# Sliding-window attention on half-array tiles: plain transposed queries, 64-row products, nine rows per partition, and one slot order for all pairs

## The chip, the core and the metric

The kernel runs on one core of one Trainium2 chip. The core has a matrix engine (TensorE; PE in the profile, PEld for its weight loads), VectorE (DVE), ScalarE (ACT), GpSimd (POOL) and a queue engine (SP). Each engine works through its own instructions in order; semaphores tie them together. 16 DMA engines move data between HBM and the core's memory SBUF. Matrix products land in PSUM, eight banks of 2 KB per partition, and VectorE and ScalarE read them from there. The metric is the device time of one execution in microseconds (us).

## What is computed

The reference is causal attention with a window of 64 positions, and behind it a mixture-of-experts layer with soft slots:

```python
# q, k, v: batch 8, heads 8, sequence 576, head size 64, fp32
scores = scale * q @ k.T                       # per batch and head
mask = (rel >= 0) & (rel < 64)                 # rel = query position - key position
attn = softmax(where(mask, scores, -1e9))
x = attn @ v                                   # -> 4608 tokens x 512
logits = x @ phi                               # 512 x 32 slots (8 experts, 4 slots each)
d = softmax(logits, over tokens)
slot_input = d.T @ x                           # 32 x 512
slot_out[e] = relu(slot_input[e] @ w1[e]) @ w2[e]     # 512 -> 1024 -> 512
out = softmax(logits, over slots) @ slot_out   # 4608 x 512, fp32
```

About 28 MB of q, k and v and 33.5 MB of weights are read, and 9.4 MB are written.

## The kernel before

**Pairs and blocks.** The 64 (batch, head) combinations are handled as 32 pairs of neighbouring heads. The sequence is cut into nine blocks of 64 queries; a block of queries sees a window of 128 keys (its own 64 and the 64 before). A window product is therefore 64 queries by 128 keys, for two heads.

**Loading and turning.** `load_rows` (L75) brings q or k of two pairs with one GpSimd DMA that casts to fp16. 96 partitions hold six consecutive rows each, four heads beside one another (RQ = 6, RP = 96). `st_transpose` (L315) turns one pair with twelve transposes of 96x64 into a PSUM bank, a_q for q and a_k for k: head 0 comes out on partitions 0 to 63 and head 1 on 64 to 127. `st_copy_k` (L325) copies k into `kT` (128 partitions by 64+576) on ScalarE, on VectorE in every fourth slot. `st_copy_q` (L332) copies q in two ScalarE instructions of 64 partitions each into `qb`, which is block diagonal: each block of 128 columns has 64 columns of head 0 (zeros on the other head's partitions) and 64 of head 1. `zero_q` writes the zeros once.

**Products.** With the block-diagonal q one 128x128 product gives both heads. `st_max` (L347) puts the mask (`wm`, by a product with the identity, two of 512 columns) and eight window products into the two banks of a_m; `st_max_read` takes the maximum of each query on VectorE. `st_max8` does the ninth block, `st_shift` turns the maxima so that they become rows of `rt`, and VectorE copies them there (L370). `st_scores` (L372) then forms the transposed scores in a_s, eight 128x128 products and eight more with `lh` and `rt` that add mask and shift; `st_exp` takes the exponential of all eight blocks in one ScalarE instruction. The ninth block has a place of its own in the bank a_k (`st_score8`, `st_exp8`). `st_av` multiplies with v, 18 products of 128x64, into a_v, and `st_norm` divides on VectorE and writes x_b.

**Behind the attention of a batch.** `fr_transpose` and `fr_transpose_copy` turn x_b into xt (PE into a_k, ScalarE out of it). After four pairs come logits (`fr_logits`, bank a_q), their running maximum (`fr_max`), exponentials (`fr_exp`), a transpose (`fr_dispatch`), the slot sums (`fr_slots`) and their accumulation (`fr_acc`, VectorE); the softmax over slots is `fr_turn`, `cb_max`, `cb_sub` (GpSimd), `cb_exp`, `cb_turn`.

**Order.** The program's order is the order on every engine. The loop over slots n = -1 to 30 handles k of pair n+1, q of pair n, maxima of n-1, shift and scores of n-2, the ninth block of n-3 and v of n-4. The work of a batch is spread by lags: in slot n the call `of(n, lag)` names the batch whose first pair is n-lag. What the last pairs still need is written out by hand behind the loop (L680 to L755). Then the experts run: `first` (L815) makes the hidden layer, `second` and `second_last` the output of the experts in two halves of 256 columns, `give` multiplies with the slot softmax, scales and writes to HBM.

**Queues.** All loads but the first rows and phi are issued by GpSimd in program order (`loads`, L542), between its own copies: `shift_v` (L176) makes a copy of v shifted by 64 rows. q and k groups have four buffers each; WSLOTS says in which slots a weight of 2 MB is issued. PSUM is used up by single buffers: a_m, a_v and a_s have two banks, a_k and a_q one, so a bank is written again only when its reader is done.

Of the kernel before, what the change touches and what calls it, by code (L numbers as in the profile page):

```python
# [18 lines left out]
def kernel(  # L19
# [47 lines left out]
    RQ = 6  # L67
    RP = S // RQ
    assert RP == 96
# [5 lines left out]
    def load_rows(src, g, tag, pairs=(0, 1)):  # L75
        t = pin.tile([128, 4, RQ * Dh], FP16, name=tag, tag=tag)
        b, gq = divmod(g, 2)
        h0, nh = 4 * gq + 2 * pairs[0], 2 * len(pairs)
        nc.gpsimd.dma_start(out=t[0:RP, 0:nh, :],  # L79
                            in_=src[b].rearrange("h (p r) d -> p h (r d)", p=RP)[:, h0:h0 + nh, :])  # L80
        for i, pr in enumerate(pairs):
            staged[tag, 2 * g + pr] = t, 2 * i
# [17 lines left out]
    for i, (src, tag, pr) in enumerate(((k, "ks", 0), (q, "qs", 0), (k, "ks", 1), (q, "qs", 1))):  # L100
        f = w1_t[5 - i // 2, 0][:, :, :].rearrange("p c f -> p (c f)").bitcast(FP32)
        f = f[0:RP, 768 * (i % 2):768 * (i % 2) + 768].rearrange("p (h x) -> p h x", h=2)
        nc.sync.dma_start(out=f, in_=src[0].rearrange("h (p r) d -> p h (r d)", p=RP)[:, 2 * pr:2 * pr + 2, :])
        if pr == 0:
            staged[tag] = pin.tile([128, 4, RQ * Dh], FP16, name=tag, tag=tag)
        first_rows[tag, pr] = f
        staged[tag, pr] = staged[tag], 2 * pr

    def round_rows(tag, pr, copy):
        copy(out=staged[tag][0:RP, 2 * pr:2 * pr + 2, :], in_=first_rows[tag, pr])  # L110
# [105 lines left out]
    NK, NQ = 4, 3  # L216
    kTs = [pqk.tile([128, 64 + S], FP16, name=f"kT{i}") for i in range(NK)]
    qbs = [pqk.tile([128, NB, 2, 64], FP16, name=f"qb{i}") for i in range(NQ)]
    def zero_q(i):
        nc.vector.memset(qbs[i][64:128, :, 0, :], 0.0)  # L220
        nc.vector.memset(qbs[i][0:64, :, 1, :], 0.0)
# [3 lines left out]
    zero_q(0)  # L225
# [16 lines left out]
    def make_rt(rt):  # L242
        nc.vector.tensor_copy(out=rt[64:128, :], in_=db[64:128, 11:12].broadcast_to([64, 128]))
        nc.vector.tensor_copy(out=rt[0:64, 0:64], in_=ident_h[0:64, 0:64])
        nc.vector.tensor_copy(out=rt[0:64, 64:128], in_=ident_h[0:64, 0:64])
# [19 lines left out]
    def late_constants(n):  # L265
        if n == 0:
            nc.vector.memset(ms[0], 0.0)
            zero_q(1)
        elif n == 1:
            nc.vector.tensor_tensor(out=lh[64:128, 0, 0:64], in0=lh[64:128, 0, 0:64],  # L270
                                    in1=db[64:128, 10:11].broadcast_to([64, 64]), op=ALU.add)
            make_rt(rts[0])
            nc.vector.memset(ms[1], 0.0)
            zero_q(2)
        elif n == 2:
            make_rt(rts[1])
        elif n == 3:
# [35 lines left out]


    def st_transpose(p, tag, tq):  # L315
        src, h = staged[tag, p]
        for r in range(RQ):
            for hf in range(2):
                nc.tensor.transpose(tq[64 * hf:64 * hf + 64, RP * r:RP * r + RP],  # L319
                                    src[0:RP, h + hf, Dh * r:Dh * r + Dh], ident_h[0:RP, 0:RP])  # L320
# [4 lines left out]
    def st_copy_k(p, on_vector=False):  # L325
        if on_vector:
            nc.vector.tensor_scalar(out=kTs[p % NK][:, 64:64 + S], in0=turned(a_kh), scalar1=QKS, scalar2=None,  # L327
                                    op0=ALU.mult)
        else:
            nc.scalar.activation(kTs[p % NK][:, 64:64 + S], turned(a_kh), AF.Copy, scale=QKS)  # L330

    def st_copy_q(p, both=False):  # L332
        for hf in range(2):
            h = slice(64 * hf, 64 * hf + 64)
            if hf and both:
                nc.vector.tensor_scalar(out=qbs[p % NQ][h, :, hf, :], in0=turned(a_qh)[h], scalar1=QKS, scalar2=None,  # L336
                                        op0=ALU.mult)
            else:
                nc.scalar.activation(qbs[p % NQ][h, :, hf, :], turned(a_qh)[h], AF.Copy, scale=QKS)  # L339

    def qblock(p, i):
        return qbs[p % NQ][:, i, :, :].rearrange("p l x -> p (l x)")

    def kwindow(p, i):
        return kTs[p % NK][:, 64 * i:64 * i + 128]

    def st_max(p):  # L347
        for j in range(2):
            nc.tensor.matmul(a_m[:, j, :], ident_h[:, :], wm[:, j:j + 4, :].rearrange("p c x -> p (c x)"),  # L349
                             start=True, stop=False, skip_group_check=True)  # L350
        for i in range(8):
            nc.tensor.matmul(a_m[:, i // 4, 128 * (i % 4):128 * (i % 4) + 128], qblock(p, i), kwindow(p, i),  # L352
                             start=False, stop=True, skip_group_check=True)
# [4 lines left out]

    m8 = a_v[:, 0, 384:512]

    def st_max8(p, m8=m8):
        nc.tensor.matmul(m8, ident_h[:, :], wm[:, 1, :], start=True, stop=False, skip_group_check=True)
        nc.tensor.matmul(m8, qblock(p, 8), kwindow(p, 8), start=False, stop=True, skip_group_check=True)

    def st_max8_read(p, m8=m8):
        nc.vector.reduce_max(ms[p % 2][:, 72:73], m8, axis=AXX)  # L366

    def st_shift(p, t_=a_v[:, 1, 384:512]):
# [3 lines left out]
    def st_scores(p, blocks, at):  # L372
        rt = rts[p % NR]
        for i in blocks:
            nc.tensor.matmul(at(i), kwindow(p, i), qblock(p, i), start=(i % 4 == 0), stop=False,  # L375
                             skip_group_check=True)
        for i in blocks:
            nc.tensor.matmul(at(i), lh[:, i, :], rt[:, :], start=False, stop=True, skip_group_check=True)  # L378

    def st_score(p):  # L380
        st_scores(p, range(8), lambda i: a_s[:, i // 4, 128 * (i % 4):128 * (i % 4) + 128])

    def st_exp(p):
        nc.scalar.activation(st_pt(p)[:, 0:8, :].rearrange("p i x -> p (i x)"), a_s[:, :, :], AF.Exp, scale=XS)  # L384

    s8 = a_k[:, 288:416]

    def st_score8(p):
        st_scores(p, (8,), lambda i: s8)

    def st_pt(p):
        if p not in pts:
            pts[p] = pw.tile([128, NB, 128], FP16, name="pt", tag="pt")
        return pts[p]

    def st_exp8(p):
        nc.scalar.activation(st_pt(p)[:, 8, :], s8, AF.Exp, scale=XS)

    def st_av(p, a_v=a_v):
# [3 lines left out]
        for hf in range(2):  # L403
            for i in range(NB):
# [4 lines left out]
                                 pt[:, i, 64 * hf:64 * hf + 64], rhs, start=True, stop=True, skip_group_check=True)  # L409

    def st_norm(p, a_v=a_v):
# [120 lines left out]
    WSLOTS = {16 * i // 5: i for i in range(10)}  # L532
    WSLOTS.update({NP - 2: 10, NP - 1: 11})

# [7 lines left out]
    def loads(n):  # L542
# [6 lines left out]
        elif i > 0:  # L549
# [5 lines left out]

    for n in range(-1, NP - 1):
        loads(n)
        lb, eb, sb, cb = [of(n, lag) for lag in range(8, 12)]
        if of(n, 12) is not None:
            cb_sub(of(n, 12), nc.gpsimd)  # L560
        def maxima():
            st_max(n - 1)
            st_max8(n - 1)
            if live(n - 2):
                st_shift(n - 2)
            st_max_read(n - 1)
            st_max8_read(n - 1)

        early = n < 4
        if live(n - 3) and not early:  # L570
            st_score8(n - 3)
        if early and live(n - 1):
            maxima()
        if n == 0:
            warm_up(1)
        if live(n - 3) and early:
            st_score8(n - 3)
        if early and live(n):
            st_transpose(n, "qs", a_qh)
            st_copy_q(n, n == 0)  # L580
        if n == 0:
            warm_up(2)
            round_rows("qs", 1, nc.scalar.copy)

        kv = n == 2 or n % 4 == 1 and not early
        if live(n + 1):
            st_transpose(n + 1, "ks", a_kh)
        if live(n - 3):
            st_exp8(n - 3)
        if live(n + 1) and not kv:  # L590
            st_copy_k(n + 1)
        if live(n - 4):
            st_av(n - 4)
        if live(n) and not early:
            st_transpose(n, "qs", a_qh)
        if lb is not None:
            fr_logits(lb)
        if live(n) and not early:
            st_copy_q(n)
        if eb is not None:  # L600
            fr_exp(eb)
        if lb is not None:
            fr_logits_copy(lb)
        if live(n - 4):
            st_norm(n - 4)
        if live(n + 1) and kv:
            st_copy_k(n + 1, True)

        if live(n - 1) and not early:
            maxima()  # L610
        if live(n - 4):
            fr_transpose(n - 4)
            fr_transpose_copy(n - 4)
        if of(n, 15) is not None:
            cb_exp(of(n, 15))
        if live(n - 2):
            st_score(n - 2)
# [352 lines left out]
```

## Time and profile before

| what | value |
|---|---|
| time, median of 3 runs | 190.93 us (190.47 to 191.08) |
| time of the profiled execution | 190.24 us |
| its span, first to last instruction | 188.2 us |
| busy: PE, DVE, ACT, POOL | 160.0, 142.9, 145.0, 83.0 us |
| granted TensorE clock, mean | 0.978 |
| read from HBM, written | 61.93 MB, 9.44 MB |
| exponentials of pairs 0, 8, 28, 31 start at | 13.80, 45.77, 130.30, 140.68 us |
| first product of the experts starts at | 150.31 us |

Busy time is a share of time with something in work, not of peak. Matrix products are pipelined: one takes some 200 ns from start to end, but the next may start 56 ns later (128 columns), so groups of products are read by the distance of their starts. The name in front of a line number is the tile that is written; "<-" in a row of waits names who ended the wait.

### The profile page before, as it was taken

What the parts mean: (1) busy time and instruction counts of PE and PEld (TensorE: products, weight loads), DVE (VectorE), ACT (ScalarE), POOL (GpSimd) and SP (SyncE); (2) the same over time, 40 slices, a digit from 0 to 9 for tenths busy, and PEclk for the clock granted to TensorE, in tenths of its full rate; (3) what the DMA queues carried; (4) which work ended last, traced back from release to release, by engine and by line L of the source; (5) the groups of instructions that cost most, each with busy time, mean ns of one, the idle gap of its engine ahead of it and who ended that gap; (6) DMA issues with size and microseconds to landing.
All of it is one profiled execution on the core that took longest, in us unless ns stands there. A gap on an engine that the chain in (4) does not pass through costs nothing.

```text
span 188.2 us, 7073 instructions
## 1 busy us (share of the span) xinstructions
PE 160.0 (85%) x3039; PEld 120.5 (64%) x3039; DVE 142.9 (76%) x354; ACT 145.0 (77%) x267; POOL 83.0 (44%) x123
## 2 busy tenths in 40 slices
PE   5777999999999999999999999999899899878400
PEld 1466778877777677777777787777785357543100
DVE  6797786897888789788888878897887734689700
ACT  6677879989889899889898898989478455589500
POOL 7955726171682453862953706707653170000000
PEclk9999999999999999999999999999999999999965
DMA  6999999999999999999999999999999999999996
GB/s 160 223 184 185 228 172 226 175 222 180 185 223 180 213 191 185 201 206 181 209 193 191 211 187 190 203 202 192 216 211 216 205 196 193 247 340 392 417 417 264
DMA packets 62302, 41.47 MB, mean 220 GB/s; under 512 B 38848, under 2 KB 58304, under 8 KB 61376
## 3 DMA queue, kind: packets, MB, share of 16 engines
q0 software_dynamic: 56560, 30.35, 116.7%
q1 hardware_dynamic: 5712, 10.68, 16.0%
q8 instruction: 23, 0.38, 0.7%
q14 instruction: 7, 0.06, 0.1%
HBM read 61.93 MB, written 9.44 MB: 379 GB/s over the span
## 4 chain that ended last, share of the span: by engine, by line
PE 45%; DVE 34%; ACT 6%; DMA 5%; issue 4%; DVEq 0%; SPq 0%; ACTq 0%
DVE m L356 10%; PE a_m L349 5%; DVE x_b L418 5%; PE a_m L352 5%; PE a_v L408 4%; PE a_s L375 4%; PE a_s L378 4%; PE a_q L319 3%; DMA out_dram<-w 3%; PE a_k L432 3%; DVE kT L327 3%; DVE rt L370 2%; DVE acc L529 2%; DMA w<-in_q_dram 2%; PE ha L819 2%
## 5 line engine op out<-in xcount | busy, mean ns | idle before, releaser
L339 ACT ACTIVATE qb<-a_q 64x576 f16<-64x576 f16 x63 | 40.6, 645 | 6.1 <-PE a_q L319 4.9
L356 DVE TENSOR_REDUCE m<-a_m 128x8 f16<-128x1024 f32 x32 | 39.1, 1223 | 1.0
L384 ACT ACTIVATE pt<-a_s 128x1024 f16<-128x1024 f32 x32 | 32.8, 1023 | 6.8 <-PE a_s L378 5.6
L183 POOL COPY v<-v 64x576 int32<-64x576 int32 x16 | 10.6, 661 | 41.1 <-DMA v<-in_v_dram 41.0
L418 DVE TENSOR_TENSOR x_b<-a_v,rc 128x640 f16<-128x640 f32 x31 | 25.6, 824 | 1.1
L352 PEld LDWEIGHTS <-qb 128*128 128x128 f16 x256 | 16.9, 98 | 7.6 <-DVE qb L336 0.3
L349 PE MATMUL a_m<-wm,ident_h 128*128 128x512 f16 x64 | 19.3, 384 | 1.4 <-DVE m L356 1.4
L378 PEld LDWEIGHTS <-lh 128*128 128x128 f16 x288 | 18.7, 98 | 2.0 <-issue 1.7
L173 POOL DMA_DIRECT2D v<-in_v_dram x16 | 19.7, 1234 | 0.0
L375 PEld LDWEIGHTS <-kT 128*128 128x128 f16 x288 | 18.6, 98 | 1.6 <-issue 1.4
L436 ACT COPY xt<-a_k 128x576 f16<-128x576 f16 x28 | 17.9, 639 | 2.2 <-PE a_k L432 0.9
L375 PE MATMUL a_s<-qb,kT 128*128 128x128 f16 x256 | 19.5, 219 | 0.0
L378 PE MATMUL a_s<-rt,lh 128*128 128x128 f16 x256 | 19.5, 219 | 0.0
L352 PE MATMUL a_m<-kT,qb 128*128 128x128 f16 x256 | 19.5, 219 | 0.0
L408 PE MATMUL a_v<-v,pt 128*64 128x65 f16 x558 | 15.6, 196 | 2.4 <-DVE m L366 1.1
L79 POOL DMA_DIRECT2D ks<-in_k_dram x15 | 10.5, 697 | 16.0 <-PE a_s L378 3.8
L370 DVE CAST rt<-a_v 9x128 f16<-9x128 f32 x30 | 8.7, 289 | 10.8 <-PE a_v L369 10.5
L408 PEld LDWEIGHTS <-pt 128*64 128x64 f16 x576 | 13.5, 110 | 4.7 <-DVE m L366 1.8
L330 ACT ACTIVATE kT<-a_k 128x576 f16<-128x576 f16 x24 | 15.7, 655 | 0.8 <-PE a_k L319 0.8
L319 PE MATMUL a_q<-ident_h,qs 96*64 96x96 f16 x384 | 14.8, 206 | 1.2 <-DVE a_q L228 1.1
L319 PE MATMUL a_k<-ident_h,ks 96*64 96x96 f16 x384 | 14.4, 212 | 1.0 <-DVE ks L110 0.8
L901 DVE TENSOR_SCALAR w<-cp,rcs 128x256 f32<-128x256 f32 (+1 forms) x24 | 13.4, 610 | 2.3 <-PE cp L896 1.9
(183 smaller groups left out, 327.8 us busy)
## 6 DMA issues: line engine op xcount, KB each, us to landing
w<-in_moe_w_dram POOLq DMA_DIRECT2D x13, 1024.0 KB, 18.0
out_dram<-w SPq DMA_DIRECT2D x8, 768.0 KB, 6.8
v<-in_v_dram POOLq DMA_DIRECT2D x16, 288.0 KB, 13.3
ks<-in_k_dram POOLq DMA_DIRECT2D x15, 288.0 KB, 15.4
qs<-in_q_dram POOLq DMA_DIRECT2D x15, 288.0 KB, 13.5
out_dram<-w SPq DMA_DIRECT2D x3, 384.0 KB, 4.0
w1h<-in_moe_w_dram POOLq DMA_DIRECT2D x4, 256.0 KB, 16.7
w<-in_moe_w_dram POOLq DMA_DIRECT2D x4, 256.0 KB, 15.3
```

What stands on the lines that cost most here:

```text
L173: nc.gpsimd.dma_start(out=v1s[b % 2][:, c, 0:Dh], in_=v[b].rearrange("h s d -> (h s) d").rearrange("(c p) d -> p c d", p=128)[:, c, :])
L319: nc.tensor.transpose(tq[64 * hf:64 * hf + 64, RP * r:RP * r + RP], src[0:RP, h + hf, Dh * r:Dh * r + Dh], ident_h[0:RP, 0:RP])
L339: nc.scalar.activation(qbs[p % NQ][h, :, hf, :], turned(a_qh)[h], AF.Copy, scale=QKS)
L349: nc.tensor.matmul(a_m[:, j, :], ident_h[:, :], wm[:, j:j + 4, :].rearrange("p c x -> p (c x)"), start=True, stop=False, skip_group_check= ...
L352: nc.tensor.matmul(a_m[:, i // 4, 128 * (i % 4):128 * (i % 4) + 128], qblock(p, i), kwindow(p, i), start=False, stop=True, skip_group_chec ...
L356: nc.vector.reduce_max(ms[p % 2][:, 64:72].rearrange("p (l c) -> p l c", l=2), a_m[:, :, :].rearrange("p l (c x) -> p l c x", x=128), axis ...
L375: nc.tensor.matmul(at(i), kwindow(p, i), qblock(p, i), start=(i % 4 == 0), stop=False, skip_group_check=True)
L378: nc.tensor.matmul(at(i), lh[:, i, :], rt[:, :], start=False, stop=True, skip_group_check=True)
L384: nc.scalar.activation(st_pt(p)[:, 0:8, :].rearrange("p i x -> p (i x)"), a_s[:, :, :], AF.Exp, scale=XS)
L408: nc.tensor.matmul(a_v[r0:r0 + 64, hf, 65 * (i // 2):65 * (i // 2) + 65], pt[:, i, 64 * hf:64 * hf + 64], rhs, start=True, stop=True, skip ...
L418: nc.vector.tensor_tensor(out=xbs[b][:, :, 128 * hp:128 * hp + 128].rearrange("p c (l d) -> p l c d", l=2), in0=avv[:, :, :, 0:64], in1=rc ...
L436: nc.scalar.copy(out=xts[b][:, hp, :], in_=th[:, 0:S])
```

## The change

Head 0 and head 1 of a pair now stay on their own 64 rows of the array in the whole attention.

- q and k: nine consecutive rows per partition (RQ = 9, RP = 64); head 0 of a pair is loaded to partitions 0 to 63 and head 1 to 64 to 127, in one DMA of 128 partitions. Turning a pair takes 18 transposes of 64x64 for q and 18 for k.
- `qT` is plain (128 partitions by 576, each head on its half) and is copied by one ScalarE instruction. k is always copied by ScalarE. Only for the ninth block GpSimd makes a small block-diagonal copy `q8` (two copies of 64x64 fp16 per pair).
- `st_max`: four mask products of 512 columns and 16 window products, each on 64 rows and 64 columns of the array; odd and even blocks go to different halves of the partitions, the heads to different banks. `st_score`: 16 products of 64 rows, 128 columns, 64 moving columns; `st_score_masks`: eight of 128x128 as before, and two for the ninth block, whose place is now in the bank a_q. `st_shift` writes into a_m. The mask product of the ninth block is split likewise.
- One loop, n = 0 to 35, holds all pairs: q and k of pair n, maxima and shift of n-1, scores and exponentials (all nine blocks) of n-2, v of n-3, `fr_transpose` of n-4. The order written out by hand for the last pairs is gone. `fr_slots` in the loop writes into a_s, and its `fr_acc` stands before the reading of the maxima; `fr_exp` comes in the slot of `fr_max`, ahead of `fr_transpose_copy` on ScalarE. Weights are issued every 3.6 slots instead of 3.2.

```diff
-    RQ = 6
+    RQ = 9
...
+    def rows_of(src, g):
+        b, gq = divmod(g, 2)
+        return src[b].rearrange("(g n l) (p r) d -> g (l p) n (r d)", g=2, l=2, r=RQ)[gq]
+
+    def load_rows(src, g, tag):
+        t = pin.tile([128, 2, RQ * Dh], FP16, name=tag, tag=tag)
+        nc.gpsimd.dma_start(out=t, in_=rows_of(src, g))
...
-    NK, NQ = 4, 3
+    NK, NQ = 3, 3
-    qbs = [pqk.tile([128, NB, 2, 64], FP16, name=f"qb{i}") for i in range(NQ)]
+    qTs = [pqk.tile([128, S], FP16, name=f"qT{i}") for i in range(NQ)]
+    q8s = [pqk.tile([128, 128], FP16, name=f"q8_{i}") for i in range(NQ)]
...
     def st_transpose(p, tag, tq):
-        src, h = staged[tag, p]
+        src = staged[tag, p]
         for r in range(RQ):
-            for hf in range(2):
-                nc.tensor.transpose(tq[64 * hf:64 * hf + 64, RP * r:RP * r + RP],
-                                    src[0:RP, h + hf, Dh * r:Dh * r + Dh], ident_h[0:RP, 0:RP])
+            for h in range(2):
+                nc.tensor.transpose(tq[half(h), 64 * r:64 * r + 64], src[half(h), Dh * r:Dh * r + Dh],
+                                    ident_h[half(h), half(h)])
...
+    def st_copy_q(p):
+        nc.scalar.activation(qTs[p % NQ][:, :], turned(a_qh), AF.Copy, scale=QKS)
+        for h in range(2):
+            nc.gpsimd.tensor_copy(out=q8s[p % NQ][half(h), half(h)].bitcast(mybir.dt.int32),
+                                  in_=qTs[p % NQ][half(h), 512:S].bitcast(mybir.dt.int32))
...
     def st_max(p):
+        for c in range(2):
+            for h in range(2):
+                nc.tensor.matmul(a_m[half(c), h, :], ident_h[half(h), half(h)],
+                                 wm[half(h), c:c + 4, :].rearrange("p c x -> p (c x)"),
+                                 start=True, stop=False, skip_group_check=True)
+        for r in range(4):
+            for c in range(2):
+                for h in range(2):
+                    nc.tensor.matmul(a_m[half(c), h, 128 * r:128 * r + 128], qblock(p, h, 2 * r + c),
+                                     kwindow(p, h, 2 * r + c), start=False, stop=True, skip_group_check=True)
...
+    def st_score(p):
+        for i in range(8):
+            for h in range(2):
+                nc.tensor.matmul(a_s[:, h, 64 * i:64 * i + 64], kwindow(p, h, i), qblock(p, h, i), start=(i == 0),
+                                 stop=False, skip_group_check=True)
+
+    def st_score_masks(p):
+        rt = rts[p % NR]
+        nc.tensor.matmul(s8, kTs[p % NK][:, 512:640], q8s[p % NQ][:, :], start=True, stop=False, skip_group_check=True)
+        nc.tensor.matmul(s8, lh[:, 8, :], rt[:, :], start=False, stop=True, skip_group_check=True)
+        for h in range(2):
+            for r in range(4):
+                nc.tensor.matmul(a_s[:, h, 128 * r:128 * r + 128], lh[:, 4 * h + r, :], rt[:, :],
+                                 start=False, stop=True, skip_group_check=True)
...
-    WSLOTS = {16 * i // 5: i for i in range(10)}
-    WSLOTS.update({NP - 2: 10, NP - 1: 11})
+    WSLOTS = {18 * i // 5: i for i in range(9)}
+    WSLOTS.update({NP - 2: 9, NP - 1: 10})
...
-    for n in range(-1, NP - 1):
+    for n in range(NP + 4):
+        loads(n)
+        if n == NP:
+            for _ in range(NKK):
+                load_last1()
+            load_w(11)
+            load_w(12)
+            make_ss4()
+            for d in range(2):
+                load_half(d)
+        lb, xb, eb, sb, cb = [of(n, lag) for lag in range(8, 13)]
+        if of(n, 13) is not None:
+            cb_sub(of(n, 13), nc.gpsimd)
...
+        if n < 2:
+            turn("ks", a_kh, st_copy_k)
...
+        turn("qs", a_qh, st_copy_q)
...
+        if xb is not None:
+            fr_logits_copy(xb)
+        if live(n - 1):
+            st_max(n - 1)
+
+        if sb is not None and sb < b - 1:
+            fr_acc(sb, fr_slots(sb, a_s[:, 0, :]))
+        if live(n - 1):
+            st_max_read(n - 1)
+        if n >= 2:
+            turn("ks", a_kh, st_copy_k)
+        if live(n - 1):
+            st_max8(n - 1)
+            st_max8_read(n - 1)
+
+        if live(n - 2):
+            st_score(n - 2)
+            st_score_masks(n - 2)
+            st_exp8(n - 2)
+            st_exp(n - 2)
+        if live(n - 4):
+            fr_transpose(n - 4)
+        if eb is not None:
+            fr_dispatch(eb)
+        if live(n - 1):
+            st_shift(n - 1)
+        if eb is not None:
+            fr_dispatch_copy(eb)
+        if xb is not None:
+            fr_max(xb)
+            fr_exp(xb)
+        if live(n - 4):
+            fr_transpose_copy(n - 4)
+
+        if lb is not None and lb < b:
+            fr_logits(lb)
+        if n == NP + 3:
+            fr_logits(b, (0, 1))
+        if live(n - 3):
+            st_av(n - 3)
+            st_norm(n - 3)
...
+        if sb is not None and sb < b - 1:
+            fr_stat(sb)
+        late_constants(n)
+
+        if of(n, 16) is not None:
+            cb_exp(of(n, 16))
+        if cb is not None:
+            fr_turn(cb)
+            cb_max(cb)
+        if of(n, 17) is not None:
+            cb_turn(of(n, 17))
```

## The prediction, made before the result was known

> **What bounds the kernel now.** I read the page first: busy shares, slices, DMA queues.
>
> ```profile
> PE 160.0 (85%) x3039; PEld 120.5 (64%) x3039; DVE 142.9 (76%) x354; ACT 145.0 (77%) x267; POOL 83.0 (44%) x123
> ...
> DMA  6999999999999999999999999999999999999996
> GB/s 160 223 184 185 228 172 226 175 222 180 185 223 180 213 191 185 201 206 181 209 193 191 211 187 190 203 202 192 216 211 216 205 196 193 247 340 392 417 417 264
> ```
>
> No engine is full, but the DMA engines are busy in every slice: loads (about 200 GB/s as written in fp16, so twice that as read) until slice 34, then output at up to 417. So two things can set the end: the attention, and the stream of loads. Next the stages: the loop, its hand-ordered end, the experts, the output.
>
> ```profile
> 21.91:130.30 108.39, 102.78 (x2164) 83.73 (x2163) 90.70 (x218) 97.85 (x178) 55.53 (x77) 1.00 1.46 197
> 130.30:150.31 20.01, 17.65 (x286) 11.78 (x282) 16.09 (x48) 12.96 (x30) 7.90 (x15) 1.00 1.13 210
> ```
>
> The columns are length, then PE, PEld, DVE, ACT, POOL. 26 slots take 108.39 us, 4.17 each; ACT is busy 90% of it, DVE 84%. Then the chain that ended last, for two slots:
>
> ```profile
> 87.25 0.29 DVE rt L370
> 87.54 0.03 issue
> 87.57 1.22 DVE m L356
> 88.79 0.20 DVE m L366
> ...
> 89.92 0.82 DVE x_b L418
> 90.75 0.67 DVE kT L327
> ```
>
> It runs through VectorE: shifted maxima, reading of the maxima, normalisation, k's copy, with PE between. Last the timeline, for rates on PE and for the end of the loads:
>
> ```profile
> 80.45 0.48 PE L408 MATMUL a_v<-v,pt 128*64 128x65 f16 x18
> 81.95 0.61 PE L352 MATMUL a_m<-kT,qb 128*128 128x128 f16 x8
> 83.80 0.22 PE L378 MATMUL a_k<-rt,lh 128*128 128x128 f16 x1
> 83.94 0.45 PE L319 MATMUL a_k<-ident_h,ks 96*64 96x96 f16 x12
> 152.49 1.52 POOL L155 DMA_DIRECT2D w2h<-in_moe_w_dram  x2 [0.94 <-DMA w1h<-in_moe_w_dram]
> 153.94 0.37 PE L677 MATMUL rp<-one,v 128*128 128x1 f16 x9
> 163.43 0.57 PE L849 MATMUL op<-w2h,hT 128*32 128x256 f16 x8
> ```
>
> Distances of starts (length less one product's own time, over the count less one): full 128 columns 56 ns (0.61 - 0.22 over 7); 65 columns on alternating column halves 16.5 ns, so two run together; small products that each load 128 columns of weights 27 ns (0.37 - 0.163 over 8). From L378 to L319 the start moves 145 ns, 90 more than 56: the price of changing the tile shape. The last weights are issued at 153.3, land 9.9 us later at the earliest, and L849 uses them at 163.4: the loads end where PE needs them.
>
> **The change, part by part, per slot.**
>
> Copies: one q copy less on ScalarE, 0.53 start to start, and k's copy from VectorE in a quarter of the slots: ACT -0.53 + 0.14, DVE -0.19 (0.746 / 4). No chain below runs through these copies, so ACT's gain counts nothing by itself.
>
> Maxima on PE: before two masks at 226 ns and eight products at 56, 0.90. Afterwards, if four quarters run together as L840's four column groups do (32 products of 256 columns in 1.05, 25 ns apart, a quarter of 112), 0.23 + 0.22 = 0.45. Row halves side by side are in no row here: the ends are 0.45 and 1.76.
>
> Scores: 0.45 before; 16 products afterwards, between 0.22 (pairs together) and 0.43 (27 ns each, as L677, whose weights also have 128 columns). I take 0.43. Masks stay at 10 x 56.
>
> Transposes: 12 at 22 ns before, 18 at 16 ns (L408, nearest in width) afterwards: +0.03 for each of q and k; the upper end, one by one at 27 ns, is +0.22 each.
> [...]
>
> Tile shape: two changes per slot before, four afterwards (64x64, 64x128, 128x128, 128x64): +0.18 at 90 ns each. For row halves no row exists; 0 to 0.15 each. The ninth block's split masks: two products more, 0 to 0.11.
>
> GpSimd: two q8 copies, nearest row L655 at 0.29 each: +0.58 per slot on an engine that is 51% busy in the loop, needed only two slots later, so nothing. But they stand behind the loads of their slot and wait for that slot's q copy, and k's load now waits for transposes of its own slot: GpSimd issues at most a slot ahead. It waited 41.0 us for v anyway. Four slots now ask for six loads of 288 KB and 1.1 weights of 1024 KB, 2.9 MB, or 15 us at 197 GB/s; at 17 us the stream has slack, so its backlog (13 to 18 us to landing) thins towards the end, worth 0 to 2 us. k and q rows are longer, 384 packets become 256 per load: 0 to -3 us of stream; I take -1. SP's first loads move the same bytes.
>
> Waits in the new order. I lay VectorE's round from one reading of the maxima to the next end to end, 0.08 for each change of engine. Plain: reading 1.14, ninth 0.28, shift on PE 0.38 with both hops, L370 0.32, v's end 0.1, reciprocal 0.24, normalisation 0.75: 3.2, some 3.4 with PE late by a little. Of four slots:
> - logits (and L462, L486): +0.7, PE behind by 0.3: 4.3.
> - maximum of logits (L456, L458, L501): +0.7 less the gap that it fills: 3.9.
> - dispatch: `fr_exp` stands ahead of the xt copy on ScalarE and waits for `fr_max`, which waits for L370. So a_k comes free late and k's transposes start 0.2 behind the reading. From there transposes 0.28, ninth 0.14, scores 0.43, masks 0.56, shape changes 0.19, L432 0.28, dispatch 0.11: shift at 2.2. L370 at 2.5, dispatch's copies until 3.2, which hold the bank a_q and with it q's transposes (3.3); transposes and maxima 0.8, slot sums until 4.8, `fr_acc` 0.8, and only then the next reading: 5.6.
> - after it: 3.4. Scores wait for `fr_acc` in a_s, inside this round.
>
> Sum 17.2. The same laying out of the old slots gives 16.8 where pairs 12 to 28 took 67.88 / 4 = 16.97, so 1% more: 17.4. With scores at 0.22 it is 17.1; with products two at a time 18.9.
>
> The sum, against the profiled span of 188.2:
> - pairs 0 to 8, with hardly any batch work: six rounds of 3.4 and two of 4.0, 28.4, against 31.97: -3.6 (ends -5 and -1.5).
> - pairs 8 to 28, five groups: 87.0 against 84.53: +2.5 (ends +1 and +10).
> - end: pairs 28 to 31 take 11.3 against 10.38, +0.9, because the hand-ordered end left `fr_slots` out of the way. From pair 31's exponential to the last L432: 1.02, `fr_exp` 0.73 and an xt copy 0.64 ahead on ScalarE, L432 0.45, v 0.7, normalisation 1.05, L432 0.45: 5.0 against 3.25, +1.7.
>
> Together +1.5. The experts follow by the same instructions (6.4 us later), the loads end near 163, under them. Profiled time 190.24 + 1.5 = 191.7; that execution lies 0.69 below the median, so as a median 190.93 + 1.5 = **192.4 us**. Own range 191.6 to 195.
>
> **The rivals.**
> - Faster. If k's transposes are not held by `fr_exp` (a free bank earlier, or ScalarE ahead by its 0.39 per slot), the 5.6 round falls to 4.2, a group to 16.0: -7 over the groups, -8 in all. Then the loads decide: they end at 163.4 less 1, the last products cannot start before, and only output of the first half can move forward: 0.5 to 3 us, 189.4. It decides once a group is under 16.6. For it: ACT is at 90% and is relieved; against it: the chain above runs through DVE and PE.
> - Tiles less together than assumed: transposes one by one +0.4 per slot, or maxima's products two at a time +0.45 per slot, partly in gaps: +4 to +8, 198. For it: no row shows row halves together. Against: L408, L840.
> [...]
> - Not together at all: maxima +1.3, transposes +0.4 per slot: +42, 233.
> - No change: the start's gain and the end's loss cancel, groups at 17.0: 190.9.
>
> **How the numbers follow.** 0.3% (0.57 us) is about what a measurement can tell from no change. Slower by the sum 0.42, tiles less together 0.13, not at all 0.04: slower 0.59. No change 0.12. Faster 0.29, bounded by the loads. The range reaches from 188.4 (loads saturated to the end) to 198.5 (tiles less together) and leaves out some 0.05 below and 0.10 above.
>
> **What would show it.** Products of st_max 14 ns apart (four together) and scores 27 ns apart; shape changes near 90 ns; PE waiting on ScalarE's xt copy at k's transposes once in four slots; readings of the maxima some 4.3, 3.9, 5.6, 3.4 apart; pair 8's exponential near 42, pair 28's near 129; the last L432 near 145.5; last weights near 163. Wrong would make me: distances of 27 or 56 ns in st_max (slower), rounds that stay under 4.2 throughout (faster), or PE waiting for w2h.

## The result, and the profile after

The changed kernel takes 219.69 us (median; 217.07 to 220.46) against 190.73 us for the kernel before: a ratio of 1.148, interval 1.139 to 1.157. Ratios and intervals, here and below, leave out slow executions (over 1.5% above the fastest of the same kernel), which the medians include. The changed kernel is slower, as forecast, but by 29 us where 1.5 were forecast, and it lies far outside the range of 188.4 to 198.5. The profiled execution took 217.07 us with a span of 214.9, 26.7 more than before's 188.2. First the page of the changed kernel: PE's busy time, the clock in 40 slices, the DMA engines, and the queue that carries instructions.

```profile
PE 158.0 (74%) x4063; PEld 120.2 (56%) x4063; DVE 136.3 (63%) x339; ACT 131.6 (61%) x242; POOL 96.6 (45%) x187
...
PEclk9958957889959999999998899999999999999965
DMA  6999999999999599999999599999999999999996
GB/s 201 173 185 217 191 213 186 192 217 186 219 152 127 80 182 177 115 143 182 161 188 171 67 118 198 101 172 85 169 208 178 218 209 196 192 319 364 411 416 268
...
q8 instruction: 31, 0.51, 1.0%
```

Every engine but GpSimd is less busy than before, PE at 74% instead of 85%: something makes all of them wait. PE has 4063 products instead of 3039, and the instruction queue moved 31 packets of 16 KB where before's page has 23:

```profile
q8 instruction: 23, 0.38, 0.7%
```

The DMA engines have dips that were not there (67 and 80 GB/s), and PE's clock is no longer full throughout. By stage (length, then PE, PEld, DVE, ACT, POOL, granted clock, DMA share, GB/s; from pair 0's exponential to pair 8's, and from there to pair 28's):

```profile
15.76:54.95 39.19, 30.15 (x872) 25.75 (x872) 22.62 (x60) 24.63 (x42) 20.95 (x42) 0.85 1.41 201
54.95:153.93 98.98, 76.70 (x2319) 62.82 (x2317) 67.66 (x155) 67.28 (x125) 48.32 (x95) 0.95 1.13 145
```

Before, the same two stages took 31.97 and 84.53 us; the second of them:

```profile
45.77:130.30 84.53, 80.06 (x1679) 64.81 (x1675) 71.04 (x165) 76.39 (x140) 45.57 (x63) 1.00 1.49 196
```

So 7.2 us come in the first eight pairs and 14.5 in the next twenty; the rest of the 26.7 is 2.0 ahead of pair 0's exponential, 0.6 from pair 28 to 31, 1.6 from there to the first expert product and 0.8 behind it. Twenty slots hold 2319 products, 116 each, and as many weight loads: 232 PE instructions per slot where 1679 products in 84.53 us make 168 before.

What PE waits for stands in the list of waits (engine, line, releaser: microseconds in total, times, longest). "issue" is time in which it waited for nothing that the profile shows.

```profile
PE a_m L354 <- issue: 5.0, 2, 2.5
PE a_q L323 <- issue: 4.4, 3, 2.1
PE a_k L323 <- ACT xt L447: 4.3, 4, 1.1
PE a_v L419 <- issue: 4.3, 3, 1.9
PE a_k L323 <- issue: 3.2, 2, 1.9
PE a_s L386 <- issue: 2.1, 1, 2.1
```

Before, the only entry of that kind for PE's products was this:

```profile
PE a_v L408 <- issue: 0.3, 1, 0.3
```

The forecast's own wait, k's transposes behind the copy of xt, is there (L447), but the gaps without a releaser are several times larger, and they sit in the middle of rows of equal products. The chain that ended last shows one of them (start, length, engine, tile and line):

```profile
56.70 0.18 PE a_m L354 x10
56.88 2.47 issue
59.35 0.37 PE a_m L354 x4
```

Most of st_max's sixteen products run, PE stands still for 2.47 us, and then the others follow, with no semaphore between them. And the timeline behind another such gap (start, length, count; idle before and its releaser in brackets):

```profile
25.95 0.35 PE L386 MATMUL a_s<-qT,kT 64*128 64x64 f16 x11
28.37 0.32 PE L386 MATMUL a_s<-qT,kT 64*128 64x64 f16 x5 [2.07 <-issue]
...
28.80 1.06 PE L396 MATMUL a_s<-rt,lh 128*128 128x128 f16 x8
...
95.25 0.61 PE L396 MATMUL a_s<-rt,lh 128*128 128x128 f16 x8
```

After the gap the eight mask products take 1.06 us instead of the 0.61 of the same row at 95.25: 107 ns apart instead of 56, with a granted clock of 0.50 from 28.4 to 34.6 us.

**Where the gaps are.** I numbered PE's recorded instructions (products, weight loads and seven others) in the order of their starts. Of the 31 places where the number is 193 beyond a multiple of 256, from 449 on, 14 hold a gap of more than 0.3 us from one start to the next, 24.9 us in all, and every gap of over 0.6 us without a semaphore ahead of it is at such a place. Between two of them goes exactly one packet of the instruction queue, 16 KB, which is 64 bytes for each of 256 instructions. Some of them (us; the block's length is from its first instruction to that of the next):

```
gap ends   block before it   packet starts    packet    end of packet   gap
at         lasted            after its start  takes     to next block
22.45      5.67              3.42             0.97      1.28            2.05
28.37      5.92              3.59             0.97      1.36            2.26
40.76      5.82              3.29             0.89      1.64            2.06
59.35      6.47              4.16             0.94      1.37            2.68
115.28     6.20              3.81             0.97      1.42            2.75
91.94      4.35              1.45             1.08      1.81            none
125.19     4.30              0.92             1.40      1.99            none
```

I read this as PE's code coming in blocks of 256 instructions; when the next block is asked for, the trace does not show. In the 14 cases with a gap the next block began 5.7 to 6.5 us after the one before it in 11 and 4.8 to 5.4 in the others. An estimate from the 5.7 to 6.5 us: 232 instructions per slot need 5.2 to 5.9 us, 168 need 3.7 to 4.3, and had 4.2. The twenty slots after pair 8 averaged 4.95, less than 5.2, because half of their blocks ended without a gap, the shortest after 4.24 us.

Before, one place of this kind holds a gap, of 0.5 us; in the changed kernel the 14 come to 24.9 us.

In the changed kernel's loop the packet tended to start later where more was moved around the block's start. Counting what the DMA engines moved from 1 us before a block's start to 2 us after it: packets that started over 3 us after the block had 154 to 219 GB/s around its start, and the three that started within 1.2 us had 17 to 91; those between had 55 to 163.

### The profile page after: what moved, and what is told of

Its sections match the earlier page's. It is cut to its first block, busy times and chain, and to the rows that moved or that the text cites. A ratio compares the mean times of both kernels' runs of the same rounds, so it can differ in the third digit from the quotient of the medians.

```text
span 214.9 us, 9127 instructions
## 1 busy us (share of the span) xinstructions
PE 158.0 (74%) x4063; PEld 120.2 (56%) x4063; DVE 136.3 (63%) x339; ACT 131.6 (61%) x242; POOL 96.6 (45%) x187
## 4 chain that ended last, share of the span: by engine, by line
PE 46%; DMA 17%; DVE 13%; issue 13%; ACT 4%; POOL 1%; SPq 1%; DVEq 0%; ACTq 0%
DMA w2h<-in_moe_w_dram 9%; PE a_s L396 6%; PE a_q L323 5%; PE a_s L386 5%; PE a_v L419 4%; PE a_k L323 4%; DMA w1h<-in_moe_w_dram 4%; PE a_k L443 3%; PE a_m L354 3%; DMA w<-in_q_dram 3%; PE a_m L348 3%; DMA out_dram<-w 2%; DVE m L358 2%; PE a_q L392 2%; DVE x_b L429 2%
## 5 line engine op out<-in xcount | busy, mean ns | idle before, releaser
L81 POOL DMA_DIRECT2D ks<-in_k_dram x15 | 10.8, 718 | 47.5 <-PE a_v L369 31.1
L333 ACT ACTIVATE qT<-a_q 128x576 f16<-128x576 f16 x32 | 20.9, 653 | 13.7 <-PE a_q L323 13.2
L447 ACT COPY xt<-a_k 128x576 f16<-128x576 f16 x32 | 20.2, 631 | 4.3 <-PE a_q L457 2.1
L323 PE MATMUL a_k<-ident_h,ks 64*64 64x64 f16 x576 | 16.6, 202 | 8.1 <-ACT xt L447 4.3
L396 PE MATMUL a_s<-rt,lh 128*128 128x128 f16 x256 | 21.9, 234 | 0.0
L323 PE MATMUL a_q<-ident_h,qs 64*64 64x64 f16 x576 | 16.9, 203 | 6.4 <-issue 4.4
L323 PEld LDWEIGHTS <-ks 64*64 64x64 f16 x576 | 14.5, 118 | 11.7 <-issue 9.8
L419 PE MATMUL a_v<-v,pt 128*64 128x65 f16 x576 | 17.4, 202 | 4.3 <-issue 4.3
L354 PEld LDWEIGHTS <-qT 64*64 64x64 f16 x512 | 16.1, 116 | 7.1 <-issue 5.7
L354 PE MATMUL a_m<-kT,qT 64*64 64x128 f16 x512 | 16.2, 231 | 5.0 <-issue 5.0
L335 POOL COPY q<-qT 64x32 int32<-64x32 int32 x64 | 13.2, 206 | 12.0 <-ACT qT L333 9.5
L396 PEld LDWEIGHTS <-lh 128*128 128x128 f16 x256 | 17.7, 106 | 1.0 <-issue 1.0
L323 PEld LDWEIGHTS <-qs 64*64 64x64 f16 x576 | 13.4, 116 | 8.0 <-issue 5.0
L443 PE MATMUL a_k<-ident_h,x_b 128*128 128x128 f16 x160 | 15.4, 231 | 2.7 <-ACT xt L447 1.5
L386 PE MATMUL a_s<-qT,kT 64*128 64x64 f16 x512 | 14.1, 197 | 4.1 <-issue 2.1
```

Of the source, the lines that this page charges most:

```text
L323: nc.tensor.transpose(tq[half(h), 64 * r:64 * r + 64], src[half(h), Dh * r:Dh * r + Dh], ident_h[half(h), half(h)])
L333: nc.scalar.activation(qTs[p % NQ][:, :], turned(a_qh), AF.Copy, scale=QKS)
L354: nc.tensor.matmul(a_m[half(c), h, 128 * r:128 * r + 128], qblock(p, h, 2 * r + c), kwindow(p, h, 2 * r + c), start=False, stop=True, skip ...
L386: nc.tensor.matmul(a_s[:, h, 64 * i:64 * i + 64], kwindow(p, h, i), qblock(p, h, i), start=(i == 0), stop=False, skip_group_check=True)
L396: nc.tensor.matmul(a_s[:, h, 128 * r:128 * r + 128], lh[:, 4 * h + r, :], rt[:, :], start=False, stop=True, skip_group_check=True)
L419: nc.tensor.matmul(a_v[r0:r0 + 64, hf, 65 * (i // 2):65 * (i // 2) + 65], pt[:, hf, 64 * i:64 * i + 64], rhs, start=True, stop=True, skip_ ...
```

## The experiments

Theory A: the supply of PE's code, held up by the loads, sets the slot. Theory B: the waits of the new order, as the forecast had them. Theory C: the small tiles do not run together after all. C falls by the trace of the changed kernel alone: its transposes start 3 and 29 ns apart in turn (16 on average), the sixteen scores 14.6, and four of st_max's products go in each 56 ns.

**Fewer instructions in the same PE time.** Two rows of one head pair in one product of 128x128:

```
-        for r in range(RQ):
-            for h in range(2):
-                nc.tensor.transpose(tq[half(h), 64 * r:64 * r + 64], src[half(h), Dh * r:Dh * r + Dh],
-                                    ident_h[half(h), half(h)])
+        for r in range(4):
+            nc.tensor.transpose(tq[:, 128 * r:128 * r + 128], src[:, 128 * r:128 * r + 128], ident_h[:, :])
+        for h in range(2):
+            nc.tensor.transpose(tq[half(h), 512:576], src[half(h), 512:576], ident_h[half(h), half(h)])
```

> The changed kernel with 12 instead of 36 transposing products per slot: two rows of one head pair in one 128x128 product, in the same bank, columns and PE time (4 x 56 ns + 2 for 18 x 16 ns). The turned q and k then hold rows of both heads mixed, so the attention is computed on other numbers; nothing else differs. Theory A (PE's code arrives in blocks of 256 instructions, some 5.9 us each while the loads saturate the DMA engines): a slot falls from 232 PE instructions to 184, its floor from 5.35 to 4.24 us, the exponential of pair 31 from 164.9 to about 150, total 198 to 206. Theory B (the new order's waits, as forecast: k's transposes behind the copy of xt): no wait is touched, 215 to 219. Theory C (small products run one by one after all): PE's time per slot is the same or 0.1 more, 215 to 221.

Measured: 202.52 us, 1.061 (1.057 to 1.065). Per tensor the six products take 0.55 us of PE (0.33 between the first starts of the two groups, 0.22 for the second) where the eighteen took 0.47, so PE has a little more to do, and yet 17 us are gone. 9 gaps are left, 8.9 us. The same two stages:

```profile
16.50:48.24 31.74, 28.36 (x680) 21.98 (x681) 22.38 (x61) 24.54 (x43) 20.13 (x39) 0.95 1.35 203
48.24:137.16 88.92, 75.66 (x1839) 57.21 (x1837) 67.43 (x154) 67.83 (x125) 48.29 (x95) 1.00 1.34 175
```

1839 products over twenty slots are 184 instructions per slot, and the clock is back at 1.00 in the second stage.

For k alone (the same lines under a condition on the tag):

> The same for k alone: 24 instead of 36 transposing products, 208 PE instructions per slot (q and k then disagree on what a partition holds, so the attention is computed on other numbers). A: halfway, floor 4.8 us, total 206 to 212. B and C: 215 to 220.

Measured: 212.48 us, 1.102 (1.094 to 1.110), 13 gaps with 14.9 us: between the two. The median is 0.5 us above what A gave; the two executions that the ratio counts, 209.25 and 211.29 us, lie inside.

**More instructions.** q's transposing products twice:

```
-        for r in range(RQ):
+        for r in 2 * list(range(RQ)) if tag == "qs" else range(RQ):
```

> The changed kernel with q's 18 transposing products issued twice per slot, with the same values: 268 PE instructions per slot. By PE's time alone 18 x 16 ns = 0.29 more per slot, at most +9: 219 to 229. Theory A: the time goes with the instructions, 4.81 x 268 / 232 = 5.56 per slot, +23: 237 to 246.

Measured: 231.29 us, 1.208 (1.199 to 1.217). The gaps grow to 22 with 35.7 us, more than PE's own 9 us, but the total is 6 us under A's: a block does not always take 5.9 us. Where the loads were thin, blocks of this kernel lasted 3.7 to 4.8 us (3.73 from 51.56 to 55.29 us, at 65 GB/s). The same for what was added to the kernel before:

```
+    def more(n):
+        for i in range(n):
+            nc.tensor.ldweights(ident_h[0:64, 0:1])
...
             st_transpose(n + 1, "ks", a_kh)
+            more(16)
```

> The kernel before with 16 loads of a single column of weights (64 x 1) added per slot behind k's transposes, 182 PE instructions instead of 166. A: there is a threshold, 4.17 us hold 181 instructions at 5.9 us per 256, so the end moves by 0 to 3 us, 191 to 194. If each instruction has a price of its own (27 ns at most, the nearest row): up to 0.43 per slot, up to 204.

Measured: 197.73 us, 1.038 (1.033 to 1.043); 5 gaps with 3.0 us. The threshold that A gave is not there in this form.

> The kernel before with 64 such loads per slot, 230 PE instructions as in the changed kernel, in the old order and with the old tiles. A: 5.3 us per slot at the loaded rate, 212 to 228, and PE stands still every 256 instructions, at the boundary, not at the added loads. If the code supply has no limit: 64 times the price of one such load, to be read in the trace from their distances, and no gaps elsewhere; 191 to 198 for prices up to 3.5 ns.

Measured: 234.4 us (two executions, 232.05 and 236.75; the trace is of the longer), and hardly a gap at the boundaries (2, with 1.2 us). In the trace such loads start 5 and 19 to 20 ns apart in turn, 12 each, so 64 are 0.8 us per slot, and the q transposes, which follow v's 18 products behind them, start 60 ns apart instead of 22. This run says what these loads cost and nothing of A: with that price most blocks last about 6 us or more anyway. The 16 at 12 ns, 0.19 per slot, explain most of the run before it as well. As a test of A both are inconclusive.

**The loads away.** The instructions of PE stay, the expert weights are asked for behind the pairs:

```
-        if n in WSLOTS:
-            load_w(WSLOTS[n])
+        pass
...
         if n == NP:
+            for i in range(11):
+                load_w(i)
```

> The changed kernel with the eleven expert weights that were loaded during the pairs (1024 KB each) asked for only after the last pair; the code and the order of all engines but GpSimd's loads stay. So the total gets longer (some 235 to 250, eleven loads of about 5 us behind the pairs), and what counts is the exponential of pair 31, at 164.9 before. Theory A (the code's blocks come late because they stand among the loads): the blocks arrive sooner after they are asked for, most gaps at the boundaries go, pair 31 at 142 to 152. Theory A2 (256 instructions take 5.9 us whatever the loads do): 162 to 166. Theory B (waits of the order): 161 to 165, since k, q and v still come in time.

Measured: the exponential of pair 31 starts at 146.46 instead of 164.88 (the total of 251.21, just above the 235 to 250 expected, has the eleven loads behind it). This is the run that decides, though it is one execution: 8134 PE instructions, the same order, the same tiles, and 18 us less. The two stages:

```profile
16.14:50.31 34.17, 27.54 (x872) 23.15 (x872) 22.64 (x60) 24.65 (x42) 19.50 (x39) 0.95 1.21 136
50.31:135.51 85.20, 73.05 (x2319) 60.07 (x2317) 67.34 (x154) 67.07 (x125) 44.20 (x88) 1.00 0.89 89
```

2319 products again, in 85.20 us instead of 98.98, at 89 GB/s instead of 145. The packets of code start 0.4 to 2 us after the start of the block ahead of them in the second stage, blocks last 3.8 to 5.7 us, and none there ends in a gap; of the five that are left (5.5 us) four lie before 39 us and one behind the pairs. That 256 instructions take 5.9 us whatever the loads do (A2) is thereby out. That q, k and v merely come sooner with the weights away does not explain it: in the changed kernel no entry of PE's waits names one of their loads. VectorE's readings of the maxima, five in a row:

```profile
104.77 1.22 DVE L358 TENSOR_REDUCE m<-a_m 128x8 f16<-128x1024 f32 x1
108.78 1.23 DVE L358 TENSOR_REDUCE m<-a_m 128x8 f16<-128x1024 f32 x1
113.07 1.22 DVE L358 TENSOR_REDUCE m<-a_m 128x8 f16<-128x1024 f32 x1
117.05 1.19 DVE L358 TENSOR_REDUCE m<-a_m 128x8 f16<-128x1024 f32 x1
122.19 1.22 DVE L358 TENSOR_REDUCE m<-a_m 128x8 f16<-128x1024 f32 x1
```

They are 4.01, 4.29, 3.98 and 5.14 apart, against the forecast 3.4, 4.3, 3.9 and 5.6 (the round of 4.01 is the first of its group; in the next group it is 3.35). A group takes 17.0 on average, 85.20 over five, against the forecast 17.4.

**The forecast's own wait.**

```
             fr_max(xb)
-            fr_exp(xb)
         if live(n - 4):
             fr_transpose_copy(n - 4)
+        if xb is not None:
+            fr_exp(xb)
```

> The changed kernel with fr_exp behind the copy of xt on ScalarE, which takes away the wait of k's transposes that I had forecast (once in four slots, 1.30 us in the trace). Theory B, the forecast's own reading: a group of four slots gets 1.3 shorter, 7 groups, 208 to 212. Theory A: the gap is time in which the next block of code arrives, which then is late by as much more: 215 to 219.

Measured: 218.61 us, 1.136 (1.127 to 1.144), which is the changed kernel within the intervals; the gaps at the boundaries are 27.3 us instead of 24.9. The wait at L447, 4.3 us in the changed kernel, is gone from PE's waits, but 2.4 us come back in the gaps, and the twenty slots after pair 8 take 98.65 us instead of 98.98. So hardly anything of the wait is won here. With the code partly out of the way:

> few_both with fr_exp behind the copy of xt. Here the code holds PE up for 8.9 us instead of 24, so the forecast's wait should be worth something: 195 to 199 against 202.5. If it is still hidden under the code: 201 to 203.

Measured: 199.63 us, 1.035 (1.024 to 1.045): 2.9 less than few_both, and the intervals of the two do not overlap. But the traces do not place the gain where the wait was. Pair 31's exponential starts at 148.19 us against 148.17 in few_both, with gaps of 13.3 us instead of 8.9; the profiled span is 2.5 us shorter, all of it behind pair 31, where the granted clock from 150 to 160 us was 0.83 instead of 0.62. So this run does not show what the wait is worth.

> weights_late with fr_exp behind the copy of xt as well: the forecast's wait with the code's delay mostly out of the way. If the wait stands on the path, as the forecast had it (5.6 forecast, 5.13 measured in weights_late for that round, 4.2 without): a group of four falls from 17.4 to 16.2 - 16.6, pair 31 from 146.5 to 139 - 142. If even here something else takes its place: 145 to 147.

Measured: pair 31 at 143.06, groups of 16.2 to 17.0 instead of 16.7 to 17.4 (16.6 on average instead of 17.0); 1 us short of what was expected for pair 31. The readings of the maxima around the dispatch are now 4.69 apart instead of 5.14, in each of the last five groups. So the wait is real and stood on the path, but less than half of its 1.1 to 1.3 us is won; the rest passes to the next thing. Both runs are single executions.

**GpSimd's loads.** k's loads one slot later, so that the queue does not stand in front of the transposes that free their buffer:

```
         if odd:
-            if 0 <= i < NG - 4:
-                load_k(i + 4)
+            pass
         elif 0 < i <= NG:
+            if 1 <= i <= NG - 4:
+                load_k(i + 3)
             shift_v(i - 1)
```

> The changed kernel with k's loads asked for one slot later, so that GpSimd no longer waits in that slot for the transposes that free their buffer (it waited 47.5 us for them in all), and v, the weights and q go out earlier. If the late loads cost time of their own: 212 to 216. Theory A: the loads only close the dips of the DMA engines and the code's blocks come as late as before or later: 217 to 222.

Measured: 220.73 us, 1.147 (1.137 to 1.157). GpSimd's waits for these buffers in the changed kernel, and in this one its longest wait and what is left of them:

```profile
POOL ks L81 <- PE a_v L369: 31.1, 8, 7.4
POOL ks L81 <- PE a_k L323: 10.5, 2, 5.6
```

```profile
POOL q L335 <- ACT qT L333: 39.5, 18, 5.4
POOL ks L81 <- PE a_v L369: 5.7, 7, 2.3
```

Over 40 us of waiting for k's buffers are gone, and the time stays. But GpSimd does not wait less: it waits 39.5 us for q's copy on ScalarE (9.5 in the changed kernel) and 25.8 us ahead of `cb_sub` (8.5), and the dips of the DMA engines remain (63 to 80 GB/s in the lowest four slices). So the run shows that moving this wait wins nothing; what loads without any wait would be worth it does not show. That the dips come from the late attention fits, but is not shown.

> few_exp_later (199.6) with k's loads a slot later too: the last weights can land earlier, since the end followed the last load by 25 us in every run so far. If GpSimd's wait holds the loads back: 194 to 198. Theory A alone: 199 to 202.

Measured: 199.21 us, 1.037 (1.030 to 1.044), no different from few_exp_later. The last load landed at 170.17 us instead of 170.85, so the weights hardly came earlier. A part of what these kernels still lose against before lies behind pair 31: from its exponential to the end few_both takes 52.6 us and before 47.5, with a granted clock of 0.62 from 150 to 160 us where before has 1.00. What lowers it there was not tested.

**A version for the kernel before.** If code is what the change pays with, one half of its layout might be had for less: q's rows nine to a partition, all else as before.

```
+        nc.gpsimd.dma_start(out=t, in_=q[b].rearrange("(g n l) (p r) d -> g (l p) n (r d)", g=2, l=2, r=9)[gq])
...
+        if h == 9:
+            for r in range(9):
+                for hf in range(2):
+                    e = slice(64 * hf, 64 * hf + 64)
+                    nc.tensor.transpose(tq[e, 64 * r:64 * r + 64], src[e, Dh * r:Dh * r + Dh], ident_h[e, e])
+            return
```

> The kernel before, with the changed kernel's layout for q's rows alone, from pair 2 on: nine rows per partition, each head on its own half of the rows, 18 transposing products of 64x64 instead of 12 of 96x64 for q. That is 12 PE instructions more per slot, 178, and q's packets are 1152 bytes written instead of 768 (the packets of k and q together took 53.8 instead of 57.0 us of sixteen engines, so some 1.5 less for q alone). Theory A with its threshold (181 instructions in 4.17 us at 5.9 per 256): the code comes just in time, the stream of loads is 1.5 shorter: 189.0 to 191.5. If the threshold is lower (the 166 already had one gap of 0.51): gaps at the boundaries of 2 to 5 us, 192 to 195.

Measured: 196.92 us, 1.032 (1.027 to 1.037). Twelve more PE instructions per slot bring 7 gaps at the boundaries, 4.4 us, and the last load lands at 163.6, not sooner than the 163.4 before. The profiled span is 6.3 us longer. So the kernel before seems to have no room for twelve more instructions per slot: in its loop most blocks already last 5.7 to 7 us, where the late blocks of the changed kernel began 4.8 to 6.5 us after the one ahead. (The version also changes tile shapes and q's copies, which were not tried by themselves.) No kernel that I ran beats it.

The runs side by side (gaps over 0.3 us at the 256 boundaries; total in us, single executions marked; the first columns are of the profiled execution):

```
                    PE instr.  gaps  sum    exp of pair 31   total
before              6085       1     0.5    140.7            190.7
before_q_nine       6445       7     4.4    146.2            196.9
few_k_load_later    6597       13    12.9   146.4            199.2
few_exp_later       6597       12    13.3   148.2            199.6
few_both            6597       9     8.9    148.2            202.5
few_k               7365       13    14.9   156.8            212.5
exp_later           8133       16    27.3   168.8            218.6
changed             8133       14    24.9   164.9            219.7
k_load_later        8133       16    24.5   164.8            220.7
q_twice             9285       22    35.7   179.8            231.3
weights_late        8134       5     5.5    146.5            251.2 (one execution)
late_exp_later      8134       5     5.8    143.1            246.7 (one execution)
```

The profiled execution of few_exp_later took 200.31 us, of 196.81 to 200.31, so its gaps are rather too many than too few.

## Why the prediction was wrong

- **The step that failed** is the one that costs the maxima, the scores and the transposes on PE. It priced products by the distances of their starts, and 32 more products per slot had no price beyond that. By my reading of the gaps, the code for the added instructions came late. Before's page shows 23 packets in the instruction queue, and the forecast quoted its DMA rows without that one. The cost is 24.9 us of gaps by the changed kernel's trace, and 18.4 us at pair 31 by weights_late. That the direction came out right is luck: the forecast's +1.5 us was a small difference of larger terms, and the 29 us come from a term that was not among them.
- **The prices on PE** were near or too high. St_max's products run four together, 14 ns apart, as taken. The scores run two together, 14.6 apart, where 27 was taken. The transposes take 16 ns, as taken. So the rival "tiles less together" has the wrong mechanism, though its sign was right. Both heads' transposes write one bank, to different partitions, and start 3 ns apart (L323 in the changed kernel). A change of tile shape cost 123 to 158 ns from start to start (medians of the four changes), near the 145 that was read from before.
- **The rounds of VectorE** were right to 0.4 us per group (weights_late), with the dispatch round at 5.14 instead of 5.6 and the round behind it at 4.01 in three groups instead of 3.4, errors that offset each other. From pair 8 to 28 it took 85.20 there against a forecast of 87.0.
- **Pairs 0 to 8** were forecast 3.6 us shorter; they are 7.2 longer. Where the code kept up, the forecast was near, and rather too long: few_both's first four slots took 12.65 us (16.50 to 29.15) against 13.6 forecast and 16.03 before. Then the gaps begin. The 2.0 us ahead of pair 0's exponential were not in the sum; the clock stands at 0.58 from 10 to 15 us there (1.00 before), and what they come from was not tried.
- **The end**: from pair 28 to 31 +0.6 (forecast +0.9), from there to the first expert product 11.27 us instead of 9.63, +1.6 (forecast +1.7). The last load lands at 189.4, not at 163, since it is asked for in step with the slots; the span ends 25.5 us after it, 24.8 before.
- **The rival "faster"** rested on k's transposes not being held by `fr_exp`. late_exp_later gives 16.6 per group without it (82.83 from pair 8 to 28, over five), where 16.0 was forecast. Before takes 16.9, so even with few gaps left the new order gains less than 0.1 us per slot there.
- **GpSimd's later loads** were costed at 0 to 2 us; k_load_later shows no gain from asking for k's loads a slot later, though GpSimd then waits elsewhere.

How the 26.7 us divide between the gaps themselves and the half clock that follows some of them was not settled: no run has the one without the other.

## What to carry to other kernels

Here smaller tiles side by side took less PE time and more PE instructions: a pair's scores went from 0.45 us (eight products, 56 ns apart) to 0.23 (sixteen, 14.6 apart), and a slot from 168 instructions to 232. Where a change does the same, count the instructions per iteration and compare the time in which 256 of them should run with the 4.8 to 6.5 us after which a late block began in the changed kernel; then look in the trace for gaps of the "issue" kind at every 256th instruction (24.9 us in the changed kernel, 0.5 before). With the weights away (weights_late, 89 GB/s instead of 145 from pair 8 to 28), as many instructions in the same order had 5.5 us of gaps. So next to loads like these I would save PE instructions before PE time: few_both has 48 fewer per slot, takes 0.55 us of PE per tensor instead of 0.47, and is 17 us shorter.

## What the runs showed of the hardware

- In the changed kernel the next 256 PE instructions began 4.8 to 6.5 us after the block ahead in the 14 blocks that ended in a gap (11 of them 5.7 to 6.5). Its shortest block in the loop took 4.24 us (146.15 to 150.39), with 61 GB/s moved meanwhile; one in q_twice took 3.73 us, with 65 GB/s.
- After or during four of the changed kernel's six gaps of over 2 us the granted clock was 0.50 for 3.4 to 6.8 us; with the other two (ending at 22.45 and 52.88 us) it stayed at 1.00. At 0.50 products of 128 columns were 107 ns apart instead of 56 (L396, 28.8 to 34.7 us).
- Products of the changed kernel on different row halves that write one PSUM bank, to different partitions, start 3 ns apart (the transposes at L323, 3 and 29 ns in turn).
- In before_more64 a load of a single weight column without a product took 12 ns in rows of 64; the twelve q transposes that follow later in the slot ran 60 ns apart instead of 22 (before), and why is open.
